# Two more token tiles transposed on TensorE, and a layer norm of four tiles moved from GpSimd to VectorE ahead of its matmuls

## The chip, the cores and the metric

One core of a Trainium2 chip. The time is that of one execution on the device, in microseconds (us); lower is better. The profile covers one execution, and its span is 1.7 to 1.8 us shorter than the time.

The engines: PE is TensorE's matmuls, PEld its weight loads, DVE is VectorE, ACT is ScalarE, POOL is GpSimd, SP only issues DMA here.

## The reference, cut

```python
x = A_x                                  # 2048 tokens x 448
xn = layernorm(x)
# mixer A: qkv, feature maps softmax(+-x @ w_phi), linear attention, @ wo
# branch B: h = gelu(xn @ w1), shifted by tokens, @ w2; x1 = xn + that
#           h2 = gelu(layernorm(x1) @ w3) @ w4
return x + A(xn) + x1 + h2
```

The kernel works on 16 token tiles of 128 tokens. A matmul contracts over partitions, so both layer norms have to be transposed: `xn` into `xnT` and, after the second layer norm (LN2), `g_tok` into `gT`.

## The kernel before

The kernel records every operation in an order of its own, works out the semaphores from the tiles that they touch, and then emits one instruction stream per engine. Order in the recording is therefore order on each engine. Because one helper emits all matmuls, nearly every PE line is L200, every DVE and POOL line L212; one tells them apart by tile names. In the profile `w` stands for several weights and small buffers, `vaug` also for scratch and the output buffer that lie in its memory, and `phik` also for the MLP's hidden layer.

PSUM is used as four pairs of banks, numbered 0 to 3. The prologue is a hand-made list in which each item names its pair:

```python
def xn_T(i, b, n=1, late=False):         # tiles i..i+n-1 through pair b
    ...                                  # 8 PE transposes of 64x128 per tile
    # then one copy per tile from PSUM into xnT: ACT, or DVE if late

play([...
      WA(0, 1), (xn_T, 6, 1), WC(0, 0), (xn_T, 7, 3), WC(0, 1), (wa_out, 0, 0), (wc_out, 0, 2),
      V(4, 0), V(6, 0), V(4, 1), (v_out, 4, 1), V(6, 1), (v_out, 6, 3),
      ...
      V(10, 0), FO(0, 0, 0), V(10, 1), (v_out, 10, 3), FO(0, 0, 1), FO(0, 2, 0), WC(2, 0), FO(0, 2, 1),
      WC(2, 1), (wc_out, 2, 0), WA(3, 0), WC(3, 0), WD(1, 0), WA(3, 1), (wa_out, 3, 2), ...])
```

`V`, `WA`, `WC`, `WD` are projections of `xnT`; a trailing 0 or 1 is the first or second half of their matmuls. `FO` folds `w_phi` into the weights of k and q, whose result DVE copies out (`wpk`, `wpq`). WA(0) works on tiles 0 to 3, WA(3) on tiles 12 to 15, which a DMA transposes.

Phase B is eight passes over pairs of tiles. `k_norm` normalizes the feature map of two tiles:

```python
def k_norm(i):
    ...
    R.ew(dve, "tensor_reduce", k, ph, axis=AX.X, op=ALU.add)          # ksum
    R.ew(dve, "reciprocal", rk, k)                                    # rks
    R.ew(pool, "tensor_tensor", ph, ph, rk..., op=ALU.mult)           # the phik multiply

for ps in range(8):
    ...
    k_norm(2 * ps)
    for i in ((), (0,), (1,), (2,), (3,), (4,), (5,), (6, 7))[ps]:
        ln_stats(st2, mv2, xn, i)                                     # LN2 statistics on DVE
ln_scale(mv2, rs2, 4, 4, 4)                                           # 1/sqrt(var) on POOL
```

Phase C is the MLP and the attention output. `a(p)`, `b(p)` are the two halves of an up-projection, followed by a gelu on ACT; `K` sums the attention state (it reads the multiplied `phik`); `A` applies LN2 on POOL, `G` transposes it by DMA. a(7) is the first that needs tiles 4 to 7. `wl[11][0]` and `w2_last` are the two halves of branch B's last w2 pair and its output; `kv_copy` (DVE) takes the attention sum out of PSUM, `kv_blocks` (PE) spreads it for `N`, the attention output of one tile:

```python
play([
    A(4, 5, 6, 7), G(4, 5, 6, 7),
    a(0), (wl[11][0],), b(0), a(1), K(10, 11), b(1), a(2), K(12, 13), b(2), a(3), K(14, 15), b(3), (kv_copy,),
    a(4), (w2_last, 11), b(4), a(5), (kv_blocks,), b(5),
    a(6), N(0), (w2_norm, 8), b(6), a(7), ...
```

The softmax here doesn't subtract the row's maximum and nothing guards it: scores larger than these inputs give would overflow.

## Time and profile before

179.34 us, the median of three runs (179.29 to 179.59).

| engine | busy us of 177.5 | role |
|---|---|---|
| PE | 168.7 | bounds the kernel; its idle time is what can be won |
| DVE | 112.1 | per tile statistics, sums, copies |
| POOL | 94.8 | multiplies, LN2 applies |
| ACT | 80.3 | exp, gelu, copies |

Two lines of the page, on busy time and on the chain of waits that ended last, by engine:

```profile
PE 168.7 (95%) x2238; PEld 90.4 (51%) x2238; DVE 112.1 (63%) x255; ACT 80.3 (45%) x91; POOL 94.8 (53%) x134
...
PE 78%; DVE 9%; POOL 5%; DMA 4%; issue 2%; SPq 1%; DVEq 0%; POOLq 0%
```

PE is on the chain for 78% of the span. The remaining 22% says where other engines hold it up. The same chain in order of time (start, length, what), cut to two places after the start:

```profile
25.04 0.66 DVE wpk L212
25.69 4.15 DMA xnT<-xn
...
29.98 40.04 PE bank L200 x560
...
71.20 1.94 DVE ksum L212
...
73.16 0.56 DVE rks L212
...
73.79 3.21 POOL phik L212
...
77.38 1.01 POOL rs L212
...
78.78 3.03 POOL g_tok L212 x4
...
83.43 2.48 DMA gT<-g_tok
...
86.00 88.73 PE bank L200 x1060
```

PE works without a break of the chain from 29.98 to 70.02 and from 86.00 to the end. Before the first of these pieces the chain leaves PE for the last DMA transpose of tiles 12 to 15, and between the two for a relay over DVE, POOL and DMA that ends when `gT` of tiles 4 to 7 lands. The view of waits says what these two cost PE (total us, times, longest):

```profile
PE bank L200 <- DMA xnT<-xn: 1.6, 1, 1.6
PE bank L200 <- DMA gT<-g_tok: 1.3, 1, 1.3
```

### The profile page before, as it was taken

What the parts mean: (1) busy time and instruction counts of PE and PEld (TensorE: products, weight loads), DVE (VectorE), ACT (ScalarE), POOL (GpSimd) and SP (SyncE); (2) the same over time, 40 slices, a digit from 0 to 9 for tenths busy, and PEclk for the clock granted to TensorE, in tenths of its full rate; (3) what the DMA queues carried; (4) which work ended last, traced back from release to release, by engine and by line L of the source; (5) the groups of instructions that cost most, each with busy time, mean ns of one, the idle gap of its engine ahead of it and who ended that gap; (6) DMA issues with size and microseconds to landing.
All of it is one profiled execution on the core that took longest, in us unless ns stands there. A gap on an engine that the chain in (4) does not pass through costs nothing.

```text
span 177.5 us, 5145 instructions
## 1 busy us (share of the span) xinstructions
PE 168.7 (95%) x2238; PEld 90.4 (51%) x2238; DVE 112.1 (63%) x255; ACT 80.3 (45%) x91; POOL 94.8 (53%) x134
## 2 busy tenths in 40 slices
PE   7799986999999999999799999999999999999993
PEld 5465664544555555454365554555545545555551
DVE  4999866149999999925756981743437416474621
ACT  2269753687877777956224421322224222224000
POOL 4775560003979999794528569470530623623740
PEclk9999999999999999999999999999999999999999
DMA  5996442125990402004111441123422220311231
GB/s 158 337 239 86 123 92 63 37 55 153 397 331 19 48 4 59 4 4 89 30 33 30 90 91 31 56 81 63 91 44 69 58 58 0 85 30 33 81 96 37
DMA packets 33766, 15.46 MB, mean 87 GB/s; under 512 B 25168, under 2 KB 33104, under 8 KB 33744
## 3 DMA queue, kind: packets, MB, share of 16 engines
q1 hardware_dynamic: 30976, 13.22, 31.5%
q10 hardware_dynamic: 2768, 1.92, 3.4%
q8 instruction: 17, 0.28, 0.6%
q14 instruction: 5, 0.04, 0.1%
HBM read 7.14 MB, written 1.84 MB: 51 GB/s over the span
## 4 chain that ended last, share of the span: by engine, by line
PE 78%; DVE 9%; POOL 5%; DMA 4%; issue 2%; SPq 1%; DVEq 0%; POOLq 0%
PE bank L200 78%; DVE st L212 3%; DMA xnT<-xn 2%; DVE xn L212 2%; POOL phik L212 2%; POOL g_tok L212 2%; DMA gT<-g_tok 1%; DVE ksum L212 1%; POOL rs L212 1%; DVE mv L212 1%; DVE wpk L212 1%; SPq L215 1%; DVE vaug L212 1%; PE bank L204 0%; DVE rks L212 0%
## 5 line engine op out<-in xcount | busy, mean ns | idle before, releaser
L208 ACT ACTIVATE phik<-bank 128x1024 bf16<-128x1024 f32 (+1 forms) x44 | 42.3, 984 | 62.7 <-PE bank L200 62.7
L200 PE MATMUL bank<-gT,w 64*128 64x512 bf16 x392 | 50.2, 377 | 1.4 <-DMA gT<-g_tok 1.3
L212 DVE TENSOR_TENSOR vaug<-bank,vaug 128x464 f32<-128x464 f32 (+3 forms) x65 | 32.6, 512 | 23.0 <-PE bank L200 21.4
L200 PE MATMUL bank<-w,phik 64*128 64x448 bf16 (+1 forms) x420 | 45.0, 349 | 0.0
L212 POOL TENSOR_TENSOR xnT<-vaug 128x196 bf16<-128x196 f32 (+1 forms) x32 | 18.1, 585 | 44.4 <-DVE vaug L212 44.4
L200 PEld LDWEIGHTS bank<-w,phik 64*128 64x128 bf16 (+1 forms) x420 | 22.1, 94 | 20.8 <-issue 0.4
L212 POOL TENSOR_TENSOR phik<-phik,rks 128x1792 bf16<-128x1792 bf16 x8 | 25.6, 3212 | 11.6 <-DVE rks L212 11.6
L200 PEld LDWEIGHTS bank<-gT,w 64*128 64x128 bf16 x392 | 17.8, 94 | 19.4 <-ACT phik L208 2.8
L212 DVE RECIPROCAL vaug<-bank 128x16 f32<-128x16 f32 x16 | 4.1, 257 | 19.4 <-PE bank L200 19.4
L212 POOL TENSOR_TENSOR vaug<-xn,xtok 128x448 f32<-128x448 bf16 x16 | 16.2, 1031 | 0.2 <-DVE vaug L212 0.2
L212 DVE TENSOR_REDUCE ksum<-phik 128x64 f32<-128x1792 bf16 x8 | 16.1, 2010 | 0.0
L200 PE MATMUL bank<-xnT,w 64*128 64x256 bf16 (+2 forms) x168 | 13.8, 307 | 1.6 <-DMA xnT<-xn 1.6
L200 PE MATMUL bank<-xnT,wpq 64*128 64x512 bf16 x112 | 14.7, 376 | 0.0
L200 PE MATMUL bank<-wv,xnT 64*128 64x448 bf16 x112 | 13.4, 350 | 0.1
L212 POOL TENSOR_TENSOR rs<-mv,mhalf 128x1 f32<-128x1 f32 (+2 forms) x19 | 12.6, 663 | 1.6
L200 PE MATMUL bank<-wo,xnT 64*128 64x448 bf16 (+1 forms) x106 | 13.4, 349 | 0.0
L200 PE MATMUL bank<-wpk,xnT 64*128 64x448 bf16 x112 | 13.2, 349 | 0.0
L200 PE MATMUL bank<-w,hT 64*128 64x448 bf16 x112 | 13.2, 349 | 0.0
L212 POOL TENSOR_SCALAR g_tok<-xn,rs 128x512 bf16<-128x512 bf16 x16 | 12.1, 767 | 0.4
L212 DVE TENSOR_TENSOR xn<-bank,xn 128x512 bf16<-128x512 f32 (+1 forms) x16 | 9.1, 614 | 1.8 <-PE bank L200 1.8
L208 ACT ACTIVATE hT<-bank 128x512 bf16<-128x512 f32 (+1 forms) x10 | 7.2, 768 | 6.2 <-PE bank L200 6.2
L212 DVE BATCH_NORM_STATS2 st<-xtok 128x6 f32<-128x448 bf16 x16 | 9.9, 616 | 0.0
(63 smaller groups left out, 163.2 us busy)
## 6 DMA issues: line engine op xcount, KB each, us to landing
w<-in_B_w_dram SPq DMA_DIRECT2D x2, 896.0 KB, 5.8
out_dram<-vaug SPq DMA_DIRECT2D x15, 112.0 KB, 1.9
w<-in_B_w_dram SPq DMA_DIRECT2D x1, 1568.0 KB, 11.1
xtok<-in_A_x_dram ACTq DMA_DIRECT2D x2, 448.0 KB, 7.6
xtok<-in_A_x_dram SPq DMA_DIRECT2D x2, 224.0 KB, 5.8
w<-in_B_w_dram ACTq DMA_DIRECT2D x2, 224.0 KB, 6.0
wo<-in_A_wo_dram SPq DMA_DIRECT2D x2, 224.0 KB, 7.0
w<-in_B_w_dram SPq DMA_DIRECT2D x1, 336.0 KB, 3.4
```

Of the source, the lines that this page charges most:

```text
L200: self.op("PE", lambda e: e.matmul(out, lhsT, rhs, start=start, stop=stop, skip_group_check=True), [out], [lhsT, rhs], tile=self._tile(lhsT))
L208: self.op("ACT", lambda e: e.activation(out, in_, func, **kw), [out], [in_] + aps)
L212: self.op(eng, lambda e: getattr(e, name)(out, *args, **kw), [out], aps)
L215: self.op(eng, lambda e: e.dma_start_transpose(out, in_), [out], [in_, *after], dma=True)
```

## The change

Its intent: take those two DMA landings off PE's path. (a) Tiles 14 and 15 are transposed on PE in place of by DMA. To have a pair for them, and to spare tile 7's transposes a wait, tiles 6 and 7 share one turn of pair 1, their copies coming after both, and other items change pair. (b) LN2 of tiles 4 to 7 is applied by DVE, right behind the last reciprocal. For that its statistics (tiles 6 and 7) and its scale come ahead of the last `k_norm`. K(12) and K(13) are drawn apart.

```diff
-            for i in range(12, NT):
+            for i in (12, 13):
                 xn_Td(i)
...
-              WA(0, 1), (xn_T, 6, 1), WC(0, 0), (xn_T, 7, 3), WC(0, 1), (wa_out, 0, 0), (wc_out, 0, 2),
+              WA(0, 1), (xn_t, 6, 1, 0), WC(0, 0), (xn_t, 7, 1, 1), (xn_e, 6, 1, 2), WC(0, 1), (wa_out, 0, 0), (wc_out, 0, 2),
...
-              V(10, 0), FO(0, 0, 0), V(10, 1), (v_out, 10, 3), FO(0, 0, 1), FO(0, 2, 0), WC(2, 0), FO(0, 2, 1),
-              WC(2, 1), (wc_out, 2, 0), WA(3, 0), WC(3, 0), WD(1, 0), WA(3, 1), (wa_out, 3, 2), WC(3, 1), (wc_out, 3, 0),
+              V(10, 0), (xn_T, 14, 3, 2), V(10, 1), (v_out, 10, 1), FO(0, 0, 0), WC(2, 0), FO(0, 0, 1), FO(0, 2, 0),
+              WC(2, 1), (wc_out, 2, 0), FO(0, 2, 1), WA(3, 0), WC(3, 0), WA(3, 1), (wa_out, 3, 2), WD(1, 0),
...
+            if ps == 7:
+                for i in (6, 7):
+                    ln_stats(st2, mv2, xn, i)
+                ln_scale(mv2, rs2, 4, 4, 0)
             k_norm(2 * ps)
-            for i in ((), (0,), (1,), (2,), (3,), (4,), (5,), (6, 7))[ps]:
-                ln_stats(st2, mv2, xn, i)
-        ln_scale(mv2, rs2, 4, 4, 4)
+            if 0 < ps < 7:
+                ln_stats(st2, mv2, xn, ps - 1)
...
-            A(4, 5, 6, 7), G(4, 5, 6, 7),
-            a(0), (wl[11][0],), b(0), a(1), K(10, 11), b(1), a(2), K(12, 13), b(2), a(3), K(14, 15), b(3), (kv_copy,),
+            *[(g_apply, i, dve) for i in (4, 5, 6, 7)], G(4, 5, 6, 7),
+            a(0), (wl[11][0],), b(0), a(1), K(10, 11), b(1), K(12), a(2), K(13), b(2), a(3), K(14, 15), b(3), (kv_copy,),
```

More of the change, by code (lines that the diff above doesn't have):

```diff
@@ L478, in fold_pair, with xn_t, xn_e @@
             return lambda: row_pairs(side(0, 0), side(1, 1), True), late
-        def xn_T(i, b, n=1, late=False):
+        def xn_t(i, b, j=0):
             t = pairs[b][:, :].bitcast(BF16).rearrange("p (h x) -> p h x", h=2)
-            for j in range(n):
-                for kc in range(KC):
-                    at = 256 * j + 64 * kc
-                    for h, (lo, hi) in enumerate((LO, HI)):
-                        R.tr(t[:, h, at:at + 64], xn[lo:hi, i + j, 128 * kc:128 * kc + 128], ident[lo:hi, lo:hi])
+            for kc in range(KC):
+                at = 256 * j + 64 * kc
+                for h, (lo, hi) in enumerate((LO, HI)):
+                    R.tr(t[:, h, at:at + 64], xn[lo:hi, i, 128 * kc:128 * kc + 128], ident[lo:hi, lo:hi])
+        def xn_e(i, b, n=1, eng="ACT"):
+            t = pairs[b][:, :].bitcast(BF16).rearrange("p (h x) -> p h x", h=2)
             for j in range(n):
@@ L489, in xn_T @@
                 fr = t[:, :, 256 * j:256 * j + 256].rearrange("p h (c e) -> p c h e", c=KC)
-                if late:
+                if eng == "ACT":
+                    R.act(to, fr, ACT.Copy)
+                else:
                     R.ew(dve, "tensor_copy", to, fr)
-                else:
-                    R.act(to, fr, ACT.Copy)
+        def xn_T(i, b, n=1, eng="ACT"):
+            for j in range(n):
+                xn_t(i + j, b, j)
+            xn_e(i, b, n, eng)
         def xn_Td(i):
@@ L654, in kv_blocks, with g_apply @@
                     R.ew(dve, "tensor_copy", dst, src)
-        def g_apply(i):
-            ln_apply(pool, halves(g_tok[:, i % 4, :]), lap(xn[:, i, :]), mv2, rs2, i)
+        def g_apply(i, eng="POOL"):
+            ln_apply(eng, halves(g_tok[:, i % 4, :]), lap(xn[:, i, :]), mv2, rs2, i)
         def g_T(i):
@@ L789, in ln1_end @@
                 ln1_apply(dve, i)
-            for i in range(12, NT):
+            for i in (12, 13):
                 xn_Td(i)
             late_3()
-        vps = {i: v_pair(i, b) for i, b in ((0, 2), (2, 3), (4, 1), (6, 3), (8, 3), (10, 3), (14, 3))}
+        vps = {i: v_pair(i, b) for i, b in ((0, 2), (2, 3), (4, 3), (6, 1), (8, 1), (10, 1), (14, 3))}
         was = {g: wa_pair(g, b) for g, b in ((0, 0), (1, 0), (2, 0), (3, 2))}
-        wcs = {g: wc_pair(g, b) for g, b in ((0, 2), (1, 1), (2, 0), (3, 0))}
+        wcs = {g: wc_pair(g, b) for g, b in ((0, 2), (1, 3), (2, 0), (3, 0))}
         wds = {h: wd_pair(h, b) for h, b in ((0, 2), (1, 3))}
-        fps = {(t, m): fold_pair(t, m, b) for t, m, b in ((1, 0, 1), (1, 2, 2), (0, 0, 2), (0, 2, 1))}
+        fps = {(t, m): fold_pair(t, m, b) for t, m, b in ((1, 0, 3), (1, 2, 2), (0, 0, 2), (0, 2, 3))}
         def V(i, k):
@@ L817, in bass_parallel_sum__linear_kernel_hedgehog__mixer_s_mlp__prompt_kernel @@
               (spin, 2, 256), V(2, 0), (v_out, 0, 2), WA(0, 0), (xn_T, 4, 1), (xn_T, 5, 2), V(2, 1), (v_out, 2, 3),
-              WA(0, 1), (xn_T, 6, 1), WC(0, 0), (xn_T, 7, 3), WC(0, 1), (wa_out, 0, 0), (wc_out, 0, 2),
-              V(4, 0), V(6, 0), V(4, 1), (v_out, 4, 1), V(6, 1), (v_out, 6, 3),
-              WA(1, 0), (xn_T, 8, 2, 2), WC(1, 0), WA(1, 1), (xn_T, 10, 3, 2, True), (ln1_end,), WC(1, 1), (wc_out, 1, 1),
-              (wa_out, 1, 0), WD(0, 0), V(8, 0), WD(0, 1), (wd_out, 0, 2), V(8, 1), (v_out, 8, 3),
+              WA(0, 1), (xn_t, 6, 1, 0), WC(0, 0), (xn_t, 7, 1, 1), (xn_e, 6, 1, 2), WC(0, 1), (wa_out, 0, 0), (wc_out, 0, 2),
+              V(4, 0), V(6, 0), V(4, 1), (v_out, 4, 3), V(6, 1), (v_out, 6, 1),
+              WA(1, 0), (xn_T, 8, 2, 2), WC(1, 0), WA(1, 1), (xn_T, 10, 1, 2, "DVE"), (ln1_end,), WC(1, 1), (wc_out, 1, 3),
+              (wa_out, 1, 0), WD(0, 0), V(8, 0), WD(0, 1), (wd_out, 0, 2), V(8, 1), (v_out, 8, 1),
               FO(1, 0, 0), WA(2, 0), FO(1, 0, 1), FO(1, 2, 0), WA(2, 1), (wa_out, 2, 0), FO(1, 2, 1),
-              V(10, 0), FO(0, 0, 0), V(10, 1), (v_out, 10, 3), FO(0, 0, 1), FO(0, 2, 0), WC(2, 0), FO(0, 2, 1),
-              WC(2, 1), (wc_out, 2, 0), WA(3, 0), WC(3, 0), WD(1, 0), WA(3, 1), (wa_out, 3, 2), WC(3, 1), (wc_out, 3, 0),
-              WD(1, 1), (wd_out, 1, 3)])
+              V(10, 0), (xn_T, 14, 3, 2), V(10, 1), (v_out, 10, 1), FO(0, 0, 0), WC(2, 0), FO(0, 0, 1), FO(0, 2, 0),
+              WC(2, 1), (wc_out, 2, 0), FO(0, 2, 1), WA(3, 0), WC(3, 0), WA(3, 1), (wa_out, 3, 2), WD(1, 0),
+              WC(3, 1), (wc_out, 3, 0), WD(1, 1), (wd_out, 1, 3)])
         for h in range(2):
```

## The prediction

> **What bounds the kernel now.** TensorE. The page gives PE 168.7 of 177.5 us busy (95%, ends modelled); the chain of waits that ended last is 78% PE. Two PE stretches make most of it: 29.98 to 70.02 and 86.00 to 174.73 us. The change aims at the holes. (1) In the chain, PE stands 28.4 to 29.98 us until the DMA transposes of tiles 12 to 15 land (waits: PE <- DMA xnT 1.6 us). Four are issued from 21.78 us, 1.27 us each, landing up to 4.2 us after issue. Before that, PE waits 0.5 us for wpk copies. (2) In the chain, ksum, rks, the last phik multiply (POOL 73.79 to 77.00), LN2 scale (to 78.7), four g_tok applies (3.03 us), transposes, gT landing at 85.91: PE waits 1.3 us. (3) At 14.2 us the transposes of tile 7 wait about 0.2 us for pair 3, which v_out(2) frees at 14.09.
>
> **Costs, A (prologue).** Two of four DMA transposes go; 16 PE transposes come, 0.41 us by the timeline, and two ACT copies of 0.6 us. The PE work falls into the 0.5 us hole before FO(0,0), ahead of which V(10) now finishes. The Trainium skill ("VectorE: DVE Perf Modes", The three transpose paths) gives 390 ns on TensorE against 1309 ns by DMA for 128x128; the trace agrees in order (0.2 us of issue, 1.27 us). WA(3) then waits for the four wpq copies (0.31 us each) and should start near 28.9 instead of 29.95: 1.0 us won. Shared turn: 0.2 us won at tile 7, while tile 6's copy comes later; ACT has the slack. A: 1.2 us (0.6 to 1.6).
>
> **Costs, B (start of phase C).** POOL loses 3.0 us of applies and a 0.2 us scale; DVE gains four applies (its bf16 128x512 one takes 0.40 us, against POOL's 0.77). But the statistics of tiles 6 and 7 now stand ahead of ksum: 1.42 us later (their stretch, 73.72 to 75.14). The phik multiply of tiles 14 and 15 moves from 77.0 to 78.4, and K(14,15), which ran at 77.64 right behind, becomes PE's new wait: about 1 us; K(12) moved into the gelu wait at 75.0 wins back 0.2. DVE applies and the POOL multiply now collide. The skill ("SBUF — State Buffer", Who interferes with whom) states an exclusive lock (agreeing: in the prologue POOL's 0.19 us operation takes 0.33 us beside an apply and ends just after it). I expect 0.4 us more on the multiply and the later applies held behind it. gT then lands at 83.4 to 85.3, before PE arrives (about 85.6), so the 1.3 us hole closes but a 1.0 to 1.5 us one opens at K(14,15). B: 0.3 us won (-1.0 to +0.7).
>
> **Time.** Later stages are PE-bound, so gains pass through whole. 179.34 - 1.2 - 0.3 = 177.8 us; range 176.7 to 178.9. Faster by over 2% 0.04, within 2% 0.94, slower 0.02.
>
> **Right or wrong in the profile.** PE <- DMA xnT gone; WA(3) about 1.2 us earlier; PE <- DMA gT gone; a new PE wait for the phik multiply near 77 to 78 us; g_tok applies on DVE 0.4 us each, or some stretched to 3 us by the lock; the stretch from a(7) to the end as long as before (88.7 us).
>
> **What would make it wrong.** Multiply not delayed (gain near 3 us); POOL locked out for all four applies (B a loss of 1 us); tiles 6 and 7's later copies stalling V(6).

## The result, and the profile after

176.88 us, the median of four runs (176.78 to 176.93), against 179.47 for four runs of before. The ratio is 0.9854 (95% interval 0.9837 to 0.9871), so 1.5% faster. Ratios here are the mean time of one kernel's runs over that of the other's of the same rounds, so not quite the ratio of the medians.

The same two lines of the page of the changed kernel:

```profile
PE 169.9 (97%) x2254; PEld 90.3 (52%) x2254; DVE 115.9 (66%) x259; ACT 81.3 (46%) x93; POOL 91.7 (52%) x129
...
PE 92%; DVE 4%; POOL 2%; issue 0%; ACT 0%; DVEq 0%
```

PE's share of the chain has gone from 78% to 92%. The chain in order of time, cut to the same two places:

```profile
25.36 0.30 PE bank L204 x15
25.66 1.34 PE bank L200 x23
...
27.02 1.29 DVE wpq L212 x4
...
28.36 40.04 PE bank L200 x557
...
69.58 0.54 DVE st L212
...
70.97 2.00 DVE ksum L212
...
72.99 0.56 DVE rks L212
...
73.62 3.23 POOL phik L212
...
76.90 95.40 PE bank L200 x1166
```

Both DMA links are gone. Where the DMA stood, PE now does the transposes itself (L204, at 25.36) and waits for four copies of `wpq` (one matmul of WA(3) runs between them, at 27.77). In the relay, the statistics (`st`, 69.58) come ahead of `ksum`, and the relay ends at the phik multiply, not at a DMA. The waits show the new one, and the tile `g_tok` shows the four DVE applies (duration in ns: minimum, median, maximum; first and last start):

```profile
PE bank L200 <- POOL phik L212: 0.7, 1, 0.7
```

```profile
L212 DVE TENSOR_SCALAR g_tok<-xn,mv,rs x4: 314/400/3301, 73.5 to 77.2; 128x512 bf16<-128x512 bf16 x4
```

One of the four applies took 3.30 us, the median was 0.40.

To size the two parts free of the start's jitter, I use two lengths within each trace. The **prologue** is the time from the first matmul of WA(0) (10.83 us before, 10.66 after, in the timeline) to the long PE piece that starts with WA(3). The **rest** is from there to the last output operation of the chain (DVE vaug, 174.76 before, 172.32 after).

| | WA(0) starts | prologue | rest |
|---|---|---|---|
| before | 10.83 | 29.98 - 10.83 = 19.15 | 174.76 - 29.98 = 144.78 |
| after | 10.66 | 28.36 - 10.66 = 17.70 | 172.32 - 28.36 = 143.96 |
| won | 0.17 | 1.45 | 0.82 |

The 0.17 us is no effect of the change: the first statistics already start that much apart (3.38 against 3.22 us), and WA(0) itself comes before any changed instruction. The change itself is thus worth 1.45 + 0.82 = 2.27 us in these traces. The experiments below test that.

### The profile page after: what moved, and what is told of

It reads as the page before. It is cut to its first block, busy times and chain, and to the rows that moved or that the text cites. A ratio compares the mean times of both kernels' runs of the same rounds, so it can differ in the third digit from the quotient of the medians.

```text
span 175.1 us, 5174 instructions
## 1 busy us (share of the span) xinstructions
PE 169.9 (97%) x2254; PEld 90.3 (52%) x2254; DVE 115.9 (66%) x259; ACT 81.3 (46%) x93; POOL 91.7 (52%) x129
## 3 DMA queue, kind: packets, MB, share of 16 engines
q10 hardware_dynamic: 2768, 1.92, 3.5%
## 4 chain that ended last, share of the span: by engine, by line
PE 92%; DVE 4%; POOL 2%; issue 0%; ACT 0%; DVEq 0%
PE bank L200 90%; POOL phik L212 2%; PE bank L204 1%; DVE ksum L212 1%; DVE wpq L212 1%; DVE xn L212 1%; DVE st L212 1%; ACT xnT L208 0%; DVE rks L212 0%; DVE vaug L212 0%; DVEq L173 0%; DVE gT L212 0%; DVE mv L212 0%
## 5 line engine op out<-in xcount | busy, mean ns | idle before, releaser
L208 ACT ACTIVATE xnT<-bank 128x512 bf16<-128x512 bf16 x12 | 6.7, 595 | 5.5 <-PE bank L204 5.3
```

Source lines behind the costliest of these rows:

```text
L208: self.op("ACT", lambda e: e.activation(out, in_, func, **kw), [out], [in_] + aps)
```

## The experiments

Each kernel gave a correct result. Twelve kernels ran, in four calls; the kernel before ran beside them (medians 179.73, 179.67, 179.38 and 179.26 us). Its runs of the first call scattered from 179.26 to 181.56 us (the slowest at a granted clock of 0.991), so effects of 0.1 to 0.2 us are read from the two lengths, not from the time. The theory: the two parts add, the prologue's is the DMA landing, and phase C's is a landing taken away for a shorter wait for the delayed multiply. Each rival stands in the expectation.

### The two parts alone

e1_prologue_only: phase B's last pass and phase C's list as before.

```diff
-            *[(g_apply, i, dve) for i in (4, 5, 6, 7)], G(4, 5, 6, 7),
+            A(4, 5, 6, 7), G(4, 5, 6, 7),          # and ln_stats, ln_scale, K as before
```

> The prologue part alone (transposes of tiles 14 and 15 on PE, shared turn of tiles 6 and 7), phase C as before. Theory (the two parts add, because everything between them is PE-bound): 1.6 us won, so about 177.8 us, and the first k matmul at about 31.9 us instead of 33.5; the hole at DMA gT stays at about 1.3 us. Rival (the prologue's 1.6 us is partly given back where phase C waits for its own POOL chain, and only the two parts together pay): under 1.0 us won and a gT hole longer than 1.5 us.

Measured: 177.90 us, ratio 0.9898. Prologue 17.70, rest 144.88, the wait for DMA gT 1.4 us. The rest is 0.10 us longer than before, with the wait for gT 0.1 us longer (one profile each). Apart from that the prologue's gain arrives whole, so the rival falls.

e2_phase_c_only: the prologue as before.

```diff
-            for i in (12, 13):
+            for i in range(12, NT):                # and the list and pairs as before
```

> Phase C's part alone, prologue as before. Theory: 0.8 us won, about 178.6 us; PE waits about 0.7 us for the phik multiply at K(14,15), one DVE apply stretched to about 3.3 us by the multiply, the multiply itself still 3.2 us, no wait for DMA gT. Rival (my prediction's 0.4 us on the multiply): multiply 3.6 us and 0.3 us won.

Measured: 178.82 us, ratio 0.9950. Prologue 19.20, rest 143.96; the wait for the multiply 0.7 us, no wait for gT, the last multiply 3.22 us against 3.21 before. The multiply is not lengthened, so the rival falls. (The page of e2 puts WA(3)'s wait down to `wpq`; in the trace's semaphores the last transpose lands after those copies, at 29.93 us, and WA(3) starts at 30.14.) The two ratios multiply to 0.9898 x 0.9950 = 0.9849, against 0.9854 for both: they add.

### What the prologue's gain is made of

e3_own_turns: tiles 6 and 7 on a pair each again; tiles 14 and 15 through pair 1.

```diff
-              (xn_t, 6, 1, 0), WC(0, 0), (xn_t, 7, 1, 1), (xn_e, 6, 1, 2), WC(0, 1)
+              (xn_T, 6, 1), WC(0, 0), (xn_T, 7, 3), WC(0, 1)     # pairs 1 and 3 exchanged elsewhere
```

> The change with tiles 6 and 7 back on a bank pair each (the numbering of before, so tiles 14 and 15 go through pair 1). Theory A (the shared turn gains at tile 7 what V(6) then loses waiting for the later copies, 0.1 us left; the rest of the 0.26 us by which the changed kernel led at 17 us came from the first tile's arrival, which varies): 0.0 to 0.15 us slower than the changed kernel, about 177.0 us. Theory B (the prediction's: the shared turn is worth 0.2 us or more): 177.1 us or more. In the trace: tile 7's transposes wait again for pair 3, and the 0.4 us wait of V(6) for ACT's copies is gone.

Measured: 177.10 us. Prologue 28.78 - 10.98 = 17.80, rest 143.96. So the shared turn is worth 0.10 us. Why so little is in the timeline. This is PE in e3, tile 7's transposes:

```profile
14.38 0.29 PE L204 MATMUL bank<-ident,xn 64*128 64x64 bf16 x8 [0.19 <-ACT vaug L208]
```

They wait for ACT's v_out of tiles 2 and 3, which holds pair 3. (The trace of before has the same 0.19 us wait at 14.23 us, put down there to a DVE statistic that neither reads nor writes what tile 7 needs; e3's record names the owner of the pair.) And this is a weight load of the changed kernel, for V(6):

```profile
15.16 1.63 PEld L200 LDWEIGHTS bank<-wv,xnT 64*128 64x128 bf16 x20 [0.42 <-ACT xnT L208]
```

Tile 7's wait is gone, but V(6) now waits for the copies of tiles 6 and 7, which start only when both are transposed.

e13_order_only: the new order and pairs, but all four tiles by DMA.

```diff
-            for i in (12, 13):
+            for i in range(12, NT):
                 xn_Td(i)
...
-              V(10, 0), (xn_T, 14, 3, 2), V(10, 1),
+              V(10, 0), V(10, 1),
```

> The changed kernel, its order of PE work and its banks, but with all four tiles 12 to 15 transposed by DMA again. Theory (the landing of the last DMA transpose, 4.1 us after its issue at 25.6 us, is what held WA(3)): WA(3) starts 19.0 us or more after WA(0), against 17.70 with the PE transposes and 19.15 in the kernel before, so at least 1.3 us of the prologue's gain is gone; time 178.1 to 178.5 us. Rival (the new order of V(10) and the folds makes a good part of the gain by itself): WA(3) starts 18.0 to 18.6 us after WA(0).

Measured: 178.38 us, ratio 0.9976 (two of its six runs were at 179.6 and 179.8 us with a granted clock of 0.989; without them the median is 178.3, and the ratio understates the gain). Prologue 29.83 - 10.79 = 19.04, rest 143.96. Its chain:

```profile
25.53 4.16 DMA xnT<-xn
...
29.83 40.04 PE bank L200 x560
```

The new order by itself, with the shared turn, wins 0.1 us. It only lengthens the wait for the DMA, from 1.6 to 2.1 us. The 1.34 us between e13 and the change (19.04 - 17.70) are the landing of the last transpose, 4.16 us after its issue. The fourth corner, the old order with the PE transposes, was not run, so what the order is worth once the DMA is gone stays open.

### What phase C's gain is made of

e5_pool_applies: statistics and scale ahead, but POOL applies (its form needs one more scale step of 0.2 us; that line is cut here).

```diff
-            *[(g_apply, i, dve) for i in (4, 5, 6, 7)], G(4, 5, 6, 7),
+            A(4, 5, 6, 7), G(4, 5, 6, 7),
```

> The change with the four LN2 applies given back to POOL, behind the phik multiply; statistics and scale stay ahead of ksum. Theory: the multiply ends as in the changed kernel (about 48.5 us after WA(3) starts), then four applies of 0.77 us, so gT lands about 0.5 us after PE gets to a(7): PE waits about 0.5 us for DMA gT besides its 0.7 us for the multiply, and the stretch from WA(3) to the last PE work grows by 0.5 us over the changed kernel's 143.96 us. Rival (the applies on DVE, held by the multiply, gain nothing over POOL's): no gT wait, stretch unchanged.

Measured: 178.36 us, ratio 0.9925. Rest 145.59: 1.63 us worse than the change, and 0.81 us worse than before. PE still waits 0.7 us for the multiply, and then:

```profile
PE bank L200 <- DMA gT<-g_tok: 1.5, 1, 1.5
```

The direction is the theory's, the size was three times mine: the four transposes are issued one behind the other from 77.80 us on, the first issue took 2.23 us against 1.19 in before (why is open), and the fourth was issued only at 82.69 us and landed 2.49 us later. So the early statistics alone would have done harm; DVE's applies pay, although one is held.

e6_stats_behind: statistics and scale behind the last `k_norm` again, applies on DVE.

```diff
-            if ps == 7:
-                for i in (6, 7):
-                    ln_stats(st2, mv2, xn, i)
-                ln_scale(mv2, rs2, 4, 4, 0)
             k_norm(2 * ps)
+            if ps == 7:
+                for i in (6, 7):
+                    ln_stats(st2, mv2, xn, i)
+                ln_scale(mv2, rs2, 4, 4, 0)
```

> The change with the statistics and the scale of tiles 4 to 7 put behind ksum and the multiply again, applies still on DVE. Theory (the statistics ahead of ksum are what delays the multiply, and without that gT comes late): multiply 1.4 us earlier, PE's wait for it gone, all four applies 0.4 us each since the multiply is over, and a wait for DMA gT of about 0.6 us in its place; stretch from WA(3) to the last PE work 143.9 us plus or minus 0.2. Rival (the multiply's delay has another cause): K(14,15) still waits for the multiply.

Measured: 177.12 us, ratio 0.9862. Rest 144.10. The four applies, now after the multiply, all took 0.41 us. The multiply starts 72.31 - 28.51 = 43.80 us after WA(3), against 73.62 - 28.36 = 45.26 in the change: 1.46 us earlier. PE no longer waits for it, and waits for gT instead:

```profile
PE bank L200 <- DMA gT<-g_tok: 0.8, 1, 0.8
```

This shows the cause of the wait for the multiply: the statistics ahead of ksum. It also shows the trade: PE waits either 0.7 us for the multiply or 0.8 us for gT.

e7_k_unsplit: K(12) and K(13) together again.

```diff
-            b(1), K(12), a(2), K(13), b(2)
+            b(1), a(2), K(12, 13), b(2)
```

> The change with K(12) and K(13) together behind a(2) again. Theory: the 0.2 us saved by K(12) in the gelu wait is lost again at K(14,15), whose start the multiply sets; so the PE wait for the multiply shrinks from 0.7 to about 0.5 us and the stretch from WA(3) to the last PE work stays at 143.96 us within 0.05. Rival (the prediction's term): 0.2 us longer, 144.16 us.

Measured: 177.10 us, ratio 0.9857. Rest 143.98, and the wait for the multiply is 0.5 us. So drawing K apart won nothing: PE comes to K(14,15) 0.2 us sooner and waits 0.2 us longer.

### The held apply, and a way past the wait

e4_k_later: K(14,15) behind b(3) and a(4).

```diff
-            a(3), K(14, 15), b(3), (kv_copy,),
-            a(4), (w2_last, 11), b(4),
+            a(3), b(3), a(4), K(14, 15), (kv_copy,),
+            (w2_last, 11), b(4),
```

> The change with K(14,15) moved behind b(3) and a(4). Theory A (only K's wait for the phik multiply is left in phase C): the wait is gone, 0.7 us won on the changed kernel, about 176.2 us. Theory B (gT, held by the three applies that the POOL multiply keeps back until 76.9 us, lands only just in time, and becomes the next wait): PE waits 0.5 to 0.8 us for DMA gT at a(7), and the time stays within 0.2 us of 176.9 us.

Measured: 176.51 us (176.19 to 176.83), ratio 0.9822. Rest 143.31, 0.65 us less than the change; no wait for the multiply, none for gT that the view of waits names. Theory A holds for the wait and the length; its 176.2 us was not reached. It is close to theory B's limit: in the trace the last `gT` lands at 83.42 us, 0.11 us before a(7)'s first weight load. The profiled run started late (WA(0) at 11.34 us), hence a span of 175.1 us.

e9_applies_first_k_later: the applies between ksum and its reciprocal, ahead of the multiply, and out of phase C's list; K and N(0) later.

```diff
             R.ew(dve, "tensor_reduce", k, ph, axis=AX.X, op=ALU.add)
+            for j in between:                      # tiles 4 to 7 in the last pass
+                g_apply(j, dve)
             R.ew(dve, "reciprocal", rk, k)
...
-            a(3), K(14, 15), b(3), (kv_copy,),
-            a(4), (w2_last, 11), b(4), a(5), (kv_blocks,), b(5),
-            a(6), N(0), (w2_norm, 8), b(6), a(7),
+            a(3), b(3),
+            a(4), (w2_last, 11), b(4), K(14, 15), (kv_copy,), a(5), b(5), (kv_blocks,),
+            a(6), b(6), N(0), (w2_norm, 8), a(7),
```

> DVE's four applies put between ksum and its reciprocal, so ahead of the multiply; K(14,15) and N(0) later on PE so as not to wait for the later multiply. Lock theory (a DVE apply that starts while the POOL multiply runs is held until it ends): all four applies take 0.3 to 0.45 us, none 3.3 us, multiply 3.2 us. Rival (the second apply waits for its scale or for its buffer): one apply is long again. Time: gT lands some 2 us before PE comes; PE waits neither for gT nor for the multiply; stretch from WA(3) to the last PE work about 143.3 us as with K moved alone, time 176.2 to 176.5 us.

Measured: 176.95 us, ratio 0.9853. The four applies:

```profile
L212 DVE TENSOR_SCALAR g_tok<-xn,mv,rs x4: 404/408/410, 73.7 to 74.7; 128x512 bf16<-128x512 bf16 x4
```

None is long. Operands and buffers are the same, only the multiply is not running, so it was the multiply that held the apply (e6 agrees). The Trainium skill ("SBUF — State Buffer", Who interferes with whom) says that VectorE in a 2-port perf mode and GpSimd lock each other out of a shared pair of ports, which fits; no run here shows the mode of the apply. The time part failed: rest 143.90, not 143.3. In its timeline PE stands neither for gT nor for the multiply; two groups of 14 matmuls, a(5) with b(5) and a(6) with b(6), took 1.91 and 1.92 us where 1.68 is usual, with weight loads idle 0.56 us for PE itself where a b half stands right behind its a half; kv_blocks waited 0.3 us for DVE. That my rearrangement of this part cost the gain is read from the trace, not tested.

e10_swap_k_w2: K(14,15) exchanged with the second half of the last w2 pair.

```diff
-            a(3), K(14, 15), b(3), (kv_copy,),
-            a(4), (w2_last, 11), b(4),
+            a(3), (w2_last, 11), b(3),
+            a(4), K(14, 15), (kv_copy,), (w2_out, 11, 2), b(4),
```

> The change with K(14,15) and the second half of the last w2 pair exchanged: the w2 half between a(3) and b(3), K behind a(4), kv_copy ahead of the w2 output on DVE. Theory (K moved alone won 0.65 us and lost about 0.2 us where b(3) came straight behind a(3) into the same banks): no wait for the multiply, no such self-wait, stretch 143.1 us (0.85 us less than the changed kernel), about 176.1 us. Rival (gT's landing, 0.1 us ahead of PE with K moved, is the next limit): a wait for DMA gT of 0.1 to 0.3 us and a stretch of 143.3 us or more.

e11_swap_two_applies_first: the same, with two applies ahead of the reciprocal (`between` of tiles 4 and 5).

> The exchange of K and the w2 half, with the applies of tiles 4 and 5 put between ksum and its reciprocal. Theory: only an apply that starts during the multiply is held, so the second is free and the third or fourth is long (about 2.9 to 3.3 us); gT lands about 1 us earlier, the multiply ends 0.7 us later, about when PE gets to K. Stretch as with the exchange alone, or 0.1 to 0.3 us less if gT was a limit there; more if the multiply is again waited for.

e12_change_again: no edit.

> The changed kernel itself once more, to stand in the same rounds as the next two. 176.8 to 177.2 us; stretch from WA(3) to the last PE work 143.96 us; ratio to before 0.985 plus or minus 0.003.

Measured in the same rounds: the change again 177.11 us (176.95 to 177.17), ratio 0.9867; e10 176.49 (176.25 to 176.81), ratio 0.9834; e11 176.48 (176.12 to 176.50), ratio 0.9828. The rest is 143.97, 143.49 and 143.29. In e12 time, prologue (17.71) and rest all repeat; its median is 179.38 - 177.11 = 2.27 us below that of before, as the two lengths said. The lengths scatter little: the prologue is 17.69 to 17.71 us in all ten profiles that have the new one, and the rest 143.96 or 143.97 us in all five with the change's phase C. Where a DMA landing sets a length, two profiles differ by 0.05 and 0.10 us (e2 and e1 against before).

e10 hit neither expectation in full: no wait for the multiply, but PE's weight loads stand 0.5 us at kv_blocks for DVE's kv_copy (in e11 too), because the w2 half no longer lies between K and kv_blocks. b(6) and a(7) on PE, from the timelines of e10 and then of e11 (start, length, operation, count):

```profile
82.42 1.87 PE L200 MATMUL bank<-gT,w 64*128 64x512 bf16 x14
```

```profile
82.59 1.68 PE L200 MATMUL bank<-gT,w 64*128 64x512 bf16 x14
```

The 0.19 us more in e10 stand at a(7), whose weight loads pause there:

```profile
83.22 0.57 PEld L200 LDWEIGHTS bank<-gT,w 64*128 64x128 bf16 x8 [0.49 <-issue]
```

The profile does not name this wait, but the trace has the landings: the last transpose was issued at 80.56 us and landed at 83.05, and a(7)'s first matmul starts at 83.25, 0.20 us later. Where the wait for gT is named, that distance is 0.09 to 0.20 us (before, e6, e1, e5). In e11 the last transpose landed at 80.77, and the pause is gone. So the rival is right there: gT is the next limit. In e11 the applies were

```profile
L212 DVE TENSOR_SCALAR g_tok<-xn,mv,rs x4: 319/410/3309, 73.2 to 74.5; 128x512 bf16<-128x512 bf16 x4
```

and the one started before the multiply (74.30 against 74.47 us) is short, while the last, started during it, is held for 3.31 us: again the lock.

e4, e10 and e11 all beat the change, by 0.4 to 0.6 us (e11 by 0.63 in the same rounds). e4 is the smallest edit: it moves one item in the list.

## Why the prediction was right or wrong

**The time.** 177.8 us was predicted and 176.88 measured, inside the range of 176.7 to 178.9 near its lower end, and within 2% as said. The gain was 1.5 us predicted; 2.27 us measured by the two lengths and by the repeat, 2.6 us by the first medians, part of which (0.17 us in the traces) was the start. Both parts were forecast too small (A by 0.25, B by 0.52 us), so the misses of the two parts did not cancel; the result lies 0.18 us from the end of the range.

**A, the prologue.** Right in mechanism, with the sum too small: 1.2 us predicted, 1.45 measured (e1: 19.15 - 17.70). "WA(3) [...] should start near 28.9": it started at 28.36, or 28.53 on the clock of before (0.17 us later). The step that failed is when the wpq copies start: 28.9 less four copies of 0.31 us puts them at 27.7, and they began at 27.02 (27.19 on that clock), no later than before (27.26). The sixteen transposes went into PE's hole of 0.48 us before FO(0,0), as the prediction said, and delayed nothing; its 28.9 is later by about their 0.41 us, as if they had to be added. "PE <- DMA xnT gone" was right. e13 puts 1.34 of the 1.45 us down to the DMA's landing. The shared turn was oversized: 0.2 predicted, 0.10 measured (e3), since V(6)'s wait, which the prediction named only as a risk ("tiles 6 and 7's later copies stalling V(6)"), takes most of it back.

**B, phase C.** 0.3 us predicted, 0.82 measured.
- "1.42 us later" for the multiply: 1.46 (e6). Right.
- "0.4 us more on the multiply": wrong, and the term that was mis-sized. The multiply took 3.22 us as ever. What was held was "the later applies", as the prediction also said: 3.30 us.
- The hole at K(14,15): 1.0 to 1.5 us predicted, 0.7 measured. Without the 0.4 us the lower end remains.
- "wins back 0.2" for K(12): not a gain of its own (e7). It arrives as a longer wait. In the sum this cancels: 1.3 - 0.7 + 0.2 = 0.8, or 1.3 - 0.5 = 0.8 with K unsplit.
- "the 1.3 us hole closes": right; PE no longer waits for gT in any trace that has the change whole.

**Gains pass through whole.** Right: e1 and e2 add up, and the PE piece after WA(3) is 40.03 or 40.04 us in every trace where the chain shows it alone. The piece from a(7) to the end, 88.7 us in the prediction, is 88.72 or 88.73 us wherever the chain shows it (before, e1, e5, e6, e10).

## What to carry to other kernels

When a relay over several engines is moved forward on an in-order engine, look at what it now stands in front of: here 1.46 us of statistics ahead of a reduction turned a wait of 1.3 us for a DMA into one of 0.7 us for a multiply, and moving one consumer back in PE's order removed that too. Work that fills an idle slot gains nothing if the next wait ends at a time that another engine sets. To size small parts, measure lengths within the traces, from one fixed instruction to another, because the start of WA(0) differed by 0.84 us between profiles of kernels whose start is the same.

## What the Trainium skill lacked or had wrong

- "SBUF — State Buffer", Who interferes with whom: the lock fits a VectorE apply that starts during a GpSimd multiply (held to 3.30 and 3.31 us, against 0.40). The page's rule that the one to issue first blocks the other fully is seen the other way round only in part. In the prologue of before it fits: GpSimd's operation of 0.19 us takes 0.34 us when it starts 0.12 us into an apply (8.63 against 8.51 us), and ends 0.05 us after that apply. But one that starts 0.05 us into an apply keeps its 0.19 us (5.25 against 5.20 us), and the multiply that starts while the first apply runs (73.62 us, the apply ending at 73.46 + 0.31 = 73.77) takes 3.22 us against 3.21 without one, not 0.15 us more. GpSimd's spans are rough, so this is open.
- "VectorE: DVE Perf Modes", The three transpose paths: 390 ns on TensorE and 1309 ns by DMA for one 128x128 block. No run here times a lone block, so these are not contradicted; they are not the costs in this stream: sixteen PE transposes of 64x128 (eight such blocks) took 0.49 us together, and a DMA transpose of 128x512 (four blocks) took 1.27 us to issue. The prediction set the page's one-block figures beside the trace's without saying that the trace's are for four.
- No page was found with the landing of a DMA transpose issued behind others. Here it was 2.4 us after issue for the first of four and 4.2 us for the last, and that landing bounded the prologue.
- No page was found with the run-to-run variation of the first input load. WA(0), which needs tiles 0 to 3, started between 10.66 and 11.50 us in the fourteen profiles; in e3, e4 and e9 the chain runs through that load (5.3 to 5.8 us from issue to landing). What set the start in the others was not looked into.
